# Reads for the range check, copies of the global keys, and the sums of second weights: three new places in the order of a sparse attention and FFN kernel

## The chip, the core and the metric

The kernel runs on one core of one Trainium2 chip. A core has TensorE (PE, with its weight loads PEld), VectorE (DVE), ScalarE (ACT), GpSimd (POOL) and SyncE (SP), which issues the DMAs here. The metric is the time of one execution on the device, in microseconds. Before the change it was 600.35 us, the median of three runs (599.40, 600.35 and 600.36). The execution that was profiled took 599.55 us.

## The reference, cut to what matters

```python
# attention: q, k, v of (4, 8, 768, 64); n_global = 8, n_local = 96
scores = np.matmul(q, k.transpose(0, 1, 3, 2)) / np.sqrt(D)
rel = pos[:, None] - pos[None, :]
is_global = pos[None, :] < n_global
is_local = (rel >= 0) & (rel < n_local)
dist = np.where(is_global & ~is_local, n_local, np.abs(rel))
scores = scores - slopes[:, None, None] * dist      # slope 2 ** -(h + 1)
a = softmax(np.where(is_global | is_local, scores, -1e9))
x = np.matmul(a, v)                                  # heads side by side: (4, 768, 512)
# feed-forward with a layer norm and a residual; w_ch1 is 512 x 2048, w_ch2 is 2048 x 512
xn = (x - mean(x)) / np.sqrt(var(x) + 1e-6) * g_ln
out = x + np.maximum(xn @ w_ch1, 0.0) @ w_ch2
```

The weights are float64 in HBM, all else is float32.

## The kernel before

**Tiles and chunks.** There are 24 tiles of 128 positions. Tiles 0 to 3 are the first tile of each batch element, tiles 4 to 8 are the other five of the first batch element in the list, and so on to tile 23. A tile's attention comes in groups of two heads, g = 0 to 3 (tiles 0 to 3 have two groups of four). Two tiles make a chunk of the feed-forward, c = 0 to 11. All float32 operands of the large products are split into a high and a low fp16 half, and a product is the sum of three fp16 products.

**The steps of a tile t, with the names that the tasks and the profile use.** S{t}_{g} on PE writes the scores (s <- kT,qT). R{t}_{g} on DVE adds the mask and takes the maxima (T <- s,mask, then nm). E on ACT takes the exponentials (mn, T). ph on ACT and pl on DVE or POOL make the two halves (pn), pt is a DMA transpose (pT <- pn), and P{t}_{g} on PE multiplies by the values (pv <- vn,pT). X divides (x <- pv,r), B squares the centred x on ACT (mean, xs), A and W on DVE and POOL make the root (rs), and C writes the centred and scaled x (xs <- x,mean,rs). xh on ACT and xl on DVE split it (xn), and xa is the DMA transpose to xT. The last 16 positions that every tile sees are the global ones: gk copies 16 columns of the first tile's keys into the block before the tile (kT <- kT on DVE), and gv does so for the values by DMA (vn <- vn).

**The steps of a chunk c.** F{c}_{f} on PE is the first product (f <- xT,w1h and w1l), G (chunks 0 to 2) and N (chunks 3 to 11) are the second. From chunk 3 on the second product is made of seven products of half size. For these, hr on ACT and hm on DVE mix the first product's results (R <- f, then R <- f,R three times), hh and hl make the halves (uh, ul), and sums of second weights are needed once: ya30, ya31, ya32 and so on add blocks of the weights (va <- va,w2l and the like) on DVE or POOL, yh and yl write the sum's halves (t <- va). There are four sets of these sums, the last digit of the key. D adds the results to x (x <- m,x), O stores them.

**The check of the weights.** After the work on tile 23 has begun, 64 reads V0 to V63 (again <- moe_w_ch, 256 KB each) bring the weights in once more, and J0 to J63 on DVE fold their exponents into one tile (seen). V{n} waits for tile 23's second scores and for a buffer; the three kinds of buffers are those of the loads (six), of the keys (three) and of the values (three). The verdict JJ follows J63, and one small product on PE (pf) takes it up near the end.

**What sets the order.** All tasks of the program are handed to a planner (`Plan`, lines 150 to 245). A task has a cost for each engine that may do it, the tasks it comes after, a rank, the buffers it takes and from which tasks they come back, and for a DMA its cost on the queue. The planner simulates the engines with these costs, and at every step takes the task that can begin first; among those that can begin within 0.05 us it takes the lowest rank. Where DVE, ACT or POOL may do a task, the one that would end it first by the planner's costs gets it. What comes out is one fixed order for each engine. On the chip every engine works through its own order, and waits at an instruction until its semaphores are reached. So one new constraint changes the choices behind it, the choice of engine too. SP waits in the same way: a read or a transpose that stands behind a waiting one is issued later. Each of SP's DMAs also waits for the landing of the eighth before it, whose semaphore it uses again.

All instructions are recorded through one helper, so every row of the profile has line L257; the names of the tiles tell them apart.

## Time and profile before

| | |
|---|---|
| median of the runs | 600.35 us |
| the profiled execution | 599.55 us, of which the span from the first to the last instruction is 597.8 us |
| TensorE | busy 586.9 us, 98% of the span, at a granted clock of 1.00 |
| VectorE | busy 494.0 us, 83% |
| ScalarE | busy 429.3 us, 72% |
| GpSimd | busy 154.0 us, 26% |
| DMA | mean 176 GB/s |

The profiled execution is 0.80 us below the median and 0.15 us above the fastest run. In a timeline row the first number is the start in us from the span's start, the second the duration, xN the instructions merged into the row, and in brackets stands how long the engine had been idle and what ended that. SPq is SP's queue: the duration of a row there is the issue of a DMA, not its transfer. The ends of matrix products are modelled, so a wait of PE of less than about 0.15 us does not show.

### The profile page before, as it was taken

The numbers are of one execution on the slowest core, as the hardware profiler recorded it, in microseconds if no ns is written. First come the engines' busy times: TensorE is split into PE (matmuls) and PEld (weight loads), VectorE is DVE, ScalarE is ACT, GpSimd is POOL, SyncE is SP. The second block draws the span as 40 slices with busy tenths as digits, with TensorE's granted clock in tenths as the row PEclk, the third lists the DMA queues.
The fourth block names the chain that finished last, engine by engine and source line by source line (L and its number), as shares of the span: only waits on it lengthen the run. The fifth ranks groups of instructions, "written<-read, shape, count | busy, mean of one in ns | idle before, by whom it ended". The sixth has DMA issues, their size and how long they took to land. (4 is left out here: it accounts for less than half of the span.)

```text
span 597.8 us, 15687 instructions
## 1 busy us (share of the span) xinstructions
PE 586.9 (98%) x5982; PEld 494.9 (83%) x5982; DVE 494.0 (83%) x1207; ACT 429.3 (72%) x1092; POOL 154.0 (26%) x133
## 2 busy tenths in 40 slices
PE   8999999999999999999999999999999999999996
PEld 5768895547956899999999999999999999888885
DVE  3899999989898987887887886877976876699994
ACT  5999697767666897797787698899686675623330
POOL 2322032135363253231330130231330420300100
PEclk9999999999999999999999999999999999999999
DMA  8995989999966848797776789759569646999931
GB/s 218 332 311 134 249 202 271 248 173 194 181 135 124 187 89 147 159 166 159 169 115 127 138 154 169 174 121 175 111 140 170 118 91 72 233 280 278 393 107 39
DMA packets 256754, 105.40 MB, mean 176 GB/s; under 512 B 238372, under 2 KB 238628, under 8 KB 256676
## 3 DMA queue, kind: packets, MB, share of 16 engines
q1 hardware_dynamic: 256672, 104.37, 78.1%
q8 instruction: 48, 0.79, 0.5%
q14 instruction: 30, 0.25, 0.1%
q10 hardware_dynamic: 4, 0.00, 0.0%
HBM read 54.53 MB, written 6.29 MB: 102 GB/s over the span
## 5 line engine op out<-in xcount | busy, mean ns | idle before, releaser
L257 PE MATMUL f<-xT,w1h 128*128 128x256 f16 x1536 | 256.3, 273 | 1.6 <-DMA xT<-xn 0.9
L257 PE MATMUL f<-xT,w1l 128*128 128x256 f16 x768 | 209.3, 273 | 0.0
L257 PEld LDWEIGHTS <-w1h 128*128 128x128 f16 x1536 | 147.3, 98 | 18.0 <-DMA xT<-xn 1.1
L257 ACT ACTIVATE uh<-R 128x896 f16<-128x896 f32 x72 | 67.9, 943 | 51.8 <-DVE R L257 50.3
L257 PEld LDWEIGHTS <-uh 128*128 128x128 f16 x1008 | 96.2, 98 | 10.5
L257 DVE SCALAR_TENSOR_TENSOR R<-f,R 128x128 f32<-128x128 f32 (+1 forms) x216 | 72.1, 334 | 20.6 <-ACT R L257 15.6
L257 PEld LDWEIGHTS <-w1l 128*128 128x128 f16 x768 | 75.1, 98 | 9.6 <-issue 0.7
L257 ACT ACTIVATE T<-T,mn 128x256 f32<-128x256 f32 x160 | 80.0, 500 | 4.3 <-ACT mn L257 0.4
L257 DVE TENSOR_TENSOR ul<-R,uh 128x896 f16<-128x896 f32 x60 | 68.1, 1136 | 17.0 <-ACT uh L257 15.9
L257 POOL TENSOR_TENSOR pn<-T,pn 128x512 f16<-128x512 f32 x37 | 49.9, 1349 | 120.2 <-ACT pn L257 82.4
L257 PE MATMUL m<-w2h,uh 128*128 128x256 f16 x288 | 78.5, 273 | 0.0
L257 PE MATMUL m<-w2l,uh 128*128 128x256 f16 x288 | 78.5, 273 | 0.0
L257 PE MATMUL m<-w2h,ul 128*128 128x256 f16 x288 | 78.5, 273 | 0.0
L257 PE MATMUL m<-t,uh 128*128 128x256 f16 x432 | 78.3, 273 | 0.0
L257 DVE CUSTOM_DVE_ANT_0 T<-s,mask 128x256 f32<-128x256 f32 (+1 forms) x192 | 68.1, 395 | 8.6 <-PE s L257 8.6
L257 PE MATMUL f<-w2h,h 128*128 128x512 f16 x192 | 60.1, 379 | 0.0
L257 PE MATMUL m<-t,ul 128*128 128x256 f16 x216 | 58.9, 273 | 0.0
L257 PE MATMUL s<-kT,qT 128*128 128x128 f16 (+1 forms) x704 | 56.9, 225 | 0.7 <-DVE kT L257 0.7
L257 PEld LDWEIGHTS <-ul 128*128 128x128 f16 x504 | 49.3, 98 | 5.7
L257 ACT ACTIVATE mn<-nm 128x2 f32<-128x2 f32 x80 | 15.8, 198 | 53.2 <-DVE nm L257 52.9
L257 POOL TENSOR_TENSOR rs<-rs,half 128x1 f32<-128x1 f32 x24 | 18.2, 760 | 138.1 <-DVE rs L257 138.0
L257 PEld LDWEIGHTS <-h 128*128 128x128 f16 x288 | 27.3, 98 | 29.7
(144 smaller groups left out, 994.6 us busy)
## 6 DMA issues: line engine op xcount, KB each, us to landing
again<-in_moe_w_ch_dram SPq DMA_DIRECT2D x64, 256.0 KB, 5.1
st<-in_moe_w_ch_dram SPq DMA_DIRECT2D x10, 1024.0 KB, 6.0
vf<-in_v_dram SPq DMA_DIRECT2D x28, 256.0 KB, 3.4
kf<-in_k_dram SPq DMA_DIRECT2D x28, 256.0 KB, 4.0
qf<-in_q_dram SPq DMA_DIRECT2D x24, 256.0 KB, 3.7
out_dram<-x SPq DMA_DIRECT2D x23, 256.0 KB, 3.6
qT<-qT SPq DMA_DIRECT2D x40, 128.0 KB, 3.5
w2h<-in_moe_w_ch_dram SPq DMA_DIRECT2D x3, 1024.0 KB, 6.6
```

Of the source, the lines that this page charges most:

```text
L257: ins = getattr(self.engine, name)(*args, **kw)
```

## The change

Three constraints of the planner are changed; no instruction is added or taken away by the diff itself.

```diff
@@ the planner's tables and Plan.task
+BEHIND = {"ya32_0": ["C5"], "yl3_0": ["C5"], "ya20_0": ["xl5"]}
...
-        self.tasks[key] = costs, fn, [a for a in after if a is not None], rank, take or {}, dma, slack, isinstance(engine, dict), port
+        self.tasks[key] = costs, fn, [a for a in [*after, *BEHIND.get(key, ())] if a is not None], rank, take or {}, dma, slack, isinstance(engine, dict), port
@@ the copy of the global keys
-                task(f"gk{b}_{i}", "DVE", 0.11, spread_k, [f"S{t - 1}_3"], rank=rank - 20, port=True)
+                task(f"gk{b}_{i}", "DVE", 0.11, spread_k, [f"S{t - 1}_3"], rank=rank - 200, port=True)
@@ the reads for the range check
-        task(f"V{n_}", "SP", 0.6, lambda n_=n_, tag=tag: read_again(n_, tag), [f"S{B * NT - 1}_1"], rank=1e4 + n_, take={tag: [f"J{n_}"]}, dma=0.8)
+        task(f"V{n_}", "SP", 0.6, lambda n_=n_, tag=tag: read_again(n_, tag), [f"S{B * NT - 1}_1"] + ([f"J{n_ - 12}"] if n_ >= 12 else []), rank=1e4 + n_, take={tag: [f"J{n_}"]}, dma=0.8, slack=2.5 * (n_ >= 12))
```

The sums ya32_0 and yl3_0 may no longer come ahead of tile 5's centred x, nor ya20_0 ahead of its low half. The copies gk get a lower rank, so they come first among what can begin. Reads from V12 on are planned 2.5 us after the J that frees their buffer.

VectorE's order from the low half of tile 6's last group on (pn6_3), before:

```order
L257 TENSOR_TENSOR pn6_3_1809<-T6_3_1749,pn6_3_1809 128x2x256
L257 TENSOR_TENSOR va0_1813<-va0_1813,w2l_86 128x512 x2
L257 TENSOR_TENSOR t3_1764<-va0_1813,t3_1764 128x2x256
L257 TENSOR_SCALAR xs5_1802<-x5_1795,mean_1803,rs_1811 128x512
L257 TENSOR_TENSOR va0_1813<-va0_1813,w2h_85 128x512
L257 TENSOR_TENSOR va0_1813<-va0_1813,w2l_86 128x512
L257 TENSOR_TENSOR xn5_1864<-xs5_1802,xn5_1864 128x512
L257 SCALAR_TENSOR_TENSOR x2_620<-f2_2_1374,x2_620 128x512
```

and now:

```order
L258 TENSOR_TENSOR pn6_3_1809<-T6_3_1750,pn6_3_1809 128x2x256
L258 TENSOR_TENSOR va0_1813<-va0_1813,w2l_86 128x512
L258 TENSOR_TENSOR va1_1845<-w2h_85 128x512
L258 TENSOR_SCALAR xs5_1802<-x5_1795,mean_1803,rs_1811 128x512
L258 TENSOR_TENSOR va0_1813<-va0_1813,w2l_86 128x512
L258 TENSOR_TENSOR xn5_1851<-xs5_1802,xn5_1851 128x512
L258 TENSOR_TENSOR t3_1762<-va0_1813,t3_1762 128x2x256
L258 TENSOR_TENSOR va0_1813<-va0_1813,w2h_85 128x512
```

The centred x of tile 5 (xs5) has moved ahead of the second addition to va0, and its low half (xn5) ahead of t3 and of two more additions. A first addition for the next set (va1), which was GpSimd's, now stands before xs5.

VectorE's order from the mixes of chunk 3's first product on (R from f1_3_0), where T9_3 is tile 9's last scores, before:

```order
L257 SCALAR_TENSOR_TENSOR R_1765<-f1_3_0_2766,R_1765 128x2x128
L257 SCALAR_TENSOR_TENSOR R_1765<-f1_3_0_2766,R_1765 128x128 x2
L257 TENSOR_TENSOR pn9_2_2833<-T9_2_2791,pn9_2_2833 128x2x256
L257 TENSOR_TENSOR w2l_86<-va2_2731,w2h_85 128x2x256
L257 TENSOR_TENSOR xn8_2804<-xs8_2715,xn8_2804 128x512
L257 ISA T9_3_2900,nm_2583<-s9_3_2863,mask1_88 128x256
L257 ISA nm_2583 128x1
L257 ISA T9_3_2900,nm_2583<-s9_3_2863,mask1_88 128x256
L257 ISA nm_2583 128x1
L257 SCALAR_TENSOR_TENSOR R_1765<-f1_3_2_2806,R_1765 128x2x128
L257 SCALAR_TENSOR_TENSOR R_1765<-f1_3_2_2806,R_1765 128x128 x2
L257 COPY kT9_1_2255<-kT09_0_2182 128x8x16
```

and now:

```order
L258 SCALAR_TENSOR_TENSOR R_1763<-f1_3_0_2749,R_1763 128x2x128
L258 SCALAR_TENSOR_TENSOR R_1763<-f1_3_0_2749,R_1763 128x128 x2
L258 TENSOR_SCALAR rs_2831<-mv_95 128x1
L258 SCALAR_TENSOR_TENSOR vn11_3_2829<-vf1_3_2774,vn11_3_2829 128x8x64
L258 COPY kT9_1_2407<-kT09_0_2171 128x8x16
L258 SCALAR_TENSOR_TENSOR R_1763<-f1_3_2_2793,R_1763 128x2x128
L258 SCALAR_TENSOR_TENSOR R_1763<-f1_3_2_2793,R_1763 128x128 x2
L258 ISA T9_3_2897,nm_2574<-s9_3_2851,mask1_88 128x256
L258 ISA nm_2574 128x1
L258 ISA T9_3_2897,nm_2574<-s9_3_2851,mask1_88 128x256
L258 ISA nm_2574 128x1
L258 TENSOR_SCALAR xs8_2819<-x8_2787,mean_2820,rs_2831 128x512
```

The mixes of the second product (R from f1_3_2) stood behind T9_3 and stand ahead of it now; halves and sums that stood between have gone elsewhere.

SP's order from the read V5 (again5) on, with tile 23's last two transposes (pT23_2 and pT23_3), before:

```order
L257 DMA again5_8465<-in_moe_w_ch1_dram 128x256
L257 DMA again12_8470<-in_moe_w_ch1_dram 128x256
L257 DMA again14_8473<-in_moe_w_ch1_dram 128x256
L257 DMA again7_8476<-in_moe_w_ch1_dram 128x256
L257 DMA_TRANSPOSE pT23_2_8489<-pn23_2_8467 128x8x128
L257 DMA again9_8521<-in_moe_w_ch1_dram 128x256
L257 DMA again13_8523<-in_moe_w_ch1_dram 128x256
L257 DMA again16_8556<-in_moe_w_ch1_dram 128x256
L257 DMA again17_8559<-in_moe_w_ch1_dram 128x256
L257 DMA again18_8569<-in_moe_w_ch1_dram 128x256
```

and now:

```order
L258 DMA again5_8465<-in_moe_w_ch1_dram 128x256
L258 DMA again7_8472<-in_moe_w_ch1_dram 128x256
L258 DMA_TRANSPOSE pT23_2_8475<-pn23_2_8467 128x8x128
L258 DMA again9_8511<-in_moe_w_ch1_dram 128x256
L258 DMA again12_8519<-in_moe_w_ch1_dram 128x256
L258 DMA again13_8521<-in_moe_w_ch1_dram 128x256
L258 DMA again14_8554<-in_moe_w_ch1_dram 128x256
L258 DMA again16_8559<-in_moe_w_ch1_dram 128x256
L258 DMA again17_8582<-in_moe_w_ch1_dram 128x256
L258 DMA out_0_dram<-x18_6721 128x512
L258 DMA again18_8613<-in_moe_w_ch1_dram 128x256
L258 DMA out_0_dram<-x19_7213 128x512
```

The transpose pT23_2 stood behind four reads and stands behind two. The reads V12 and V14 have moved behind it, and all that stood ahead of pT23_3 still does.

Of the tasks that the diff does not name, 30 change between DVE and POOL, all between the sums of the first set and tile 10. From tile 7's third scores to the mixes of chunk 3's first product DVE gains 15 tasks (ya41_0, yl4_0, ya31_2, ya32_2, yl3_2, kl10_2, pl8_1, ya30_3, ya41_2, ya10_0, ya10_2, yl3_3, ya12_2, yl1_2, ya21_3) and loses 10 (pl7_1, ql9, kl9_1, pl8_0, ya20_2, yl2_2, C7, A8, C8, kl11_3), some to POOL, some to an earlier or later place on DVE. POOL has three tensor operations fewer there. On PE the products P8 and P9 stand one place later among the larger ones, so P9_1 now follows the third product of chunk 3 (F3_4) instead of preceding it.

## Rows read from the trace of the kernel before

**Rows 1.** The page's head and its first part: busy us, share, instructions.

```profile
span 597.8 us, 15687 instructions
...
PE 586.9 (98%) x5982; PEld 494.9 (83%) x5982; DVE 494.0 (83%) x1207; ACT 429.3 (72%) x1092; POOL 154.0 (26%) x133
```

**Rows 2.** Waits of PE: us in total, times, longest us.

```profile
PE pv L257 <- DMA pT<-pn: 1.0, 2, 0.5
PE f L257 <- DMA xT<-xn: 0.9, 1, 0.9
PE s L257 <- DVE kT L257: 0.7, 1, 0.7
```

**Rows 3.** Timeline around the copy of the global keys for tile 6.

```profile
110.70 0.42 DVE L257 CUSTOM_DVE_ANT_0 T<-s,mask 128x256 f32<-128x256 f32 x1
...
111.39 0.19 DVE L257 COPY kT<-kT 128x128 f16<-128x128 f16 x1
...
111.64 0.22 PE L257 MATMUL s<-kT,qT 128*128 128x128 f16 x1 [0.70 <-DVE kT L257]
```

**Rows 4.** Timeline from tile 5's centred x to chunk 2's first product.

```profile
129.75 2.25 DVE L257 TENSOR_TENSOR va<-va,w2l 128x512 f32<-128x512 f32 x2
...
133.29 0.54 DVE L257 TENSOR_SCALAR xs<-x,mean,rs 128x512 f32<-128x512 f32 x1
...
133.87 0.63 ACT L257 ACTIVATE xn<-xs 128x512 f16<-128x512 f32 x1 [1.22 <-DVE xs L257]
...
135.08 0.68 DVE L257 TENSOR_TENSOR xn<-xs,xn 128x512 f16<-128x512 f32 x1
...
135.79 1.23 SPq L257 DMA_TRANSPOSE xT<-xn  x1
...
140.50 0.39 PE L257 MATMUL f<-xT,w1h 128*128 128x256 f16 x2 [0.93 <-DMA xT<-xn]
```

**Rows 5.** Windows: us, busy of PE, PEld, DVE, ACT, POOL, then clock, DMA.

```profile
144.10:195.20 51.10, 51.10 (x496) 37.35 (x495) 46.95 (x98) 36.37 (x103) 24.14 (x20) 1.00 0.82 158
```

**Rows 6.** Groups on DVE, 144.1 to 195.2: busy us, mean ns, idle before.

```profile
L257 DVE TENSOR_TENSOR va<-va,w2l 128x512 f32<-128x512 f32 x8 | 7.3, 913 | 0.1
L257 DVE TENSOR_TENSOR pn<-T,pn 128x512 f16<-128x512 f32 x7 | 7.1, 1019 | 1.3 <-ACT pn L257 1.2
```

**Rows 7.** Timeline of DVE, PE and ACT at chunk 3's first mixes.

```profile
195.19 1.07 DVE L257 SCALAR_TENSOR_TENSOR R<-f,R 128x256 f32<-128x256 f32 x3
...
198.67 1.07 DVE L257 SCALAR_TENSOR_TENSOR R<-f,R 128x256 f32<-128x256 f32 x3
...
197.85 0.58 ACT L257 ACTIVATE R<-f 128x512 f32<-128x512 f32 x1
...
196.32 0.39 PE L257 MATMUL f<-xT,w1h 128*128 128x256 f16 x2
...
198.95 0.38 PE L257 MATMUL f<-xT,w1h 128*128 128x256 f16 x2
```

**Rows 8.** Timeline of SP's queue and PE at tile 23's transposes.

```profile
518.76 2.75 SPq L257 DMA_DIRECT2D again<-in_moe_w_ch_dram  x4
521.61 1.30 SPq L257 DMA_TRANSPOSE pT<-pn  x1
...
528.45 1.28 SPq L257 DMA_TRANSPOSE pT<-pn  x1
...
525.85 0.52 PE L257 MATMUL pv<-vn,pT 128*128 128x64 f16 x12 [0.49 <-DMA pT<-pn]
...
533.58 0.52 PE L257 MATMUL pv<-vn,pT 128*128 128x64 f16 x12
```

**Rows 9.** Windows, columns as in rows 5: DMA share and GB/s come last.

```profile
526.00:529.00 3.00, 3.00 (x38) 2.72 (x36) 2.76 (x8) 0.00 (x0) 0.00 (x0) 1.00 1.01 307
```

**Rows 10.** Timeline of the verdict's last step on DVE and PE's product.

```profile
579.30 0.16 DVE L257 TENSOR_REDUCE mask<-ok 128x1 f32<-128x8 f32 x1
...
584.16 0.21 PE L257 MATMUL pf<-mask,ones 128*1 128x27 f32 x2
```

## The prediction

> **What bounds the kernel now.** I read the page's first part first: PE is busy in 98% of the span, 586.9 of 597.8 us [rows 1], so only what PE waits for can be won. The windows next: in the two stretches quoted here PE is busy from end to end, at a granted clock of 1.00, the 2.4 GHz level [rows 5, 9], and the windows over the rest of the span after the start read the same, so the clock has nothing to give back. Then the waits of PE. After the start-up the table holds four: 0.70 us once for DVE's copy of the global keys, 0.93 once for a transpose xT, and two of nearly 0.5 for transposes pT [rows 2]. They add up to 2.6 us, 0.4% of the time, and each of the three edits aims at one kind. The two pT waits belong to tile 23, one for its second group of two heads and one for its third [rows 8]. So the whole change has a ceiling of 2.6 us, and the question is what the moved instructions make late in exchange. The profiled run took 599.55 us, 1.75 more than its span and 0.80 less than the median of 600.35; I take gains from the profile and set them against the median.
>
> **Copies of the global keys.** Before tile 6's scores, DVE's order has two custom operations of tile 5's last range (T from s) and then the copy; the first begins at 110.70, the copy runs at 111.39 for 0.19, and PE goes on at 111.64 after 0.70 idle [rows 3]. With the copy first, it can begin at 110.70, so PE goes on at 110.95: 0.69 of the 0.70 is gained. The two custom operations end 0.19 later; behind them on DVE queue the next halves, and ACT's exponentials wait for them, but no wait of PE for pT shows there [rows 2]. Bounds: 0.5 (if the copy's input, not its place, held it by 0.2) to 0.70; taken 0.70. The copies of the other tiles have no wait in PE's table, so earlier or later they are worth 0 until one falls behind its scores.
>
> **The centred x of tile 5.** In the trace DVE runs the last two additions to va as one row of 2.25 us from 129.75, then a half (t), then xs at 133.29, 0.54 long; ACT makes the high half after 1.22 idle, DVE the low half at 135.08 for 0.68, SP issues the transpose at 135.79, and PE takes it up at 140.50 after 0.93 idle [rows 4]. Ahead of xs now goes one addition fewer (2.25 / 2 = 1.1), and t (1.1 between 132.0 and 133.29), and one first addition more (0.7 to 0.9 by [rows 6]): xs moves 1.3 to 1.5 earlier if its inputs are there. The low half then has one addition behind xs, not two, and waits for ACT's high half (0.63, [rows 4]), which begins with xs done. In all the issue comes 1.4 to 2.8 earlier. From the issue at 135.79 to PE's start passes 4.7 us; with the first edit's 0.70 PE wants the product at 140.50 - 0.93 - 0.70 = 138.9, and the transpose is there at 137.7 to 139.1. So the 0.93 goes, but for 0.2 at the worst end. Bounds 0.7 to 0.93, taken 0.93; the two edits give **1.63**, if nothing behind gives it back.
>
> **What the planner moves with it.** The thirty tasks that change between DVE and GpSimd are the dearest part. From 144.1 to 195.2 DVE is busy 46.95 of 51.10 us [rows 5], 4.15 idle. It gains 15 tasks there, mostly halves and additions, and loses 10. Such tasks last 0.68 alone (the low half in [rows 4]) and 0.91 to 1.02 on the mean in this stretch [rows 6], where GpSimd runs 20 operations beside them. Five more at 0.66 to 0.84 are 3.3 to 4.2 us. Against that GpSimd does three tensor operations fewer; if what the means lie above 0.68 comes from running beside it, each of its operations costs DVE 0.25 to 0.5, so 0.7 to 1.5 come back. Net +1.8 to +3.5 us of work, 2.6 between them. All of it must be done before the first mixes of chunk 3 (R from f, 1.07 at 195.19), whose bank PE wants at 196.32 [rows 7]. In the new order PE is 1.63 ahead, and the product P9_1 (twelve products, about 0.4 of PE's time by [rows 8]) has gone behind; so the bank is wanted at 196.32 - 1.63 - 0.4 = 194.3, and DVE must begin by 193.2. The stretch also begins earlier, at 144.1 - 1.3 = 142.8, since its first operation follows scores of PE (two tasks, 0.3 us by their overlap, now stand ahead of it). So 46.95 + 2.6 = 49.55 us of work stand in 50.4 us, and 0.85 of the 4.15 us of idle time may stay; 1.65 with the small end, nothing with the large one. The moved additions and halves of weights wait for nothing on PE, and some of the idle time is a wait for ACT (1.3 in front of the seven low halves, [rows 6]) in which they fit. Bounds: a loss of 0 (the idle time fills) to 4.2 (all stays, with the large end). Taken **0**, also because up to 0.7 lost here would be lost right behind it anyway:
>
> There the order of VectorE has tile 9's last range (T9_3) behind the second mixes instead of ahead of them, and the range frees the bank for the product that PE begins at 198.95, now wanted at 197.3 [rows 7]. The mixes wait for ACT's part (R from f at 197.85, 0.58 long [rows 7]), which ended at 198.43. By its order ACT loses two halves and a mask's copy ahead of that part and gains a square: about one half less, 0.63 [rows 4]. So the part ends at 196.2 if it also follows PE's 1.63, and at 197.8 if ACT stays where it was. Behind it come the mixes, 1.07, and the range, two custom operations of 0.42 less an overlap of some 0.05: the bank is free at 198.0 to 199.6, and PE is held for 0.7 to 2.3; 0 if the halves on ACT turn out 0.7 earlier still, as they do when VectorE's previous range comes early. Taken **-0.7**, the case in which ACT follows PE, because its input is PE's; 0.1 more for the third product's bank.
>
> **Reads for the range check.** SP's queue issues four reads in 2.75 us from 518.76, 0.69 each, before the third transpose at 521.61 [rows 8]. Two of them now stand behind it, so it goes out 1.38 us earlier and lands that much earlier: its wait of 0.49 [rows 8] is gone. The second transpose's 0.46 stays, since ahead of it nothing changes. But the two reads have only moved behind the third transpose and still stand ahead of the fourth, which goes out at 528.45 [rows 8]; around it the DMA engines are at a share of 1.01, 307 GB/s [rows 9]. So the same bytes land before it, at the same time. PE took its fourth group at 533.58 with no wait that shows [rows 8]; arriving there 0.49 earlier, it waits 0.49. Net 0 (0 to 0.5), taken **0**. The trace says transfers come one after another there; that is what the 0 hangs on. The Trainium skill ("DMA: Bandwidth & Descriptors", section "Queues, rings and completion order") says that a later transfer may end before an earlier one, since completion isn't first in, first out per queue. By that rule the fourth transpose needn't wait for the moved reads' bytes, and the 0.49 would be kept; no row here shows one overtaking. At the end, the verdict's step on DVE is done at 579.46 and PE's product on it begins at 584.16 [rows 10]: 4.7 us cover what later reads delay there, so that costs 0, and would cost what exceeds 4.7.
>
> **Sum.** 0.70 + 0.93 - 0.70 - 0.10 + 0 = 0.83 us: 598.7 for a run like the profiled one, **599.5** against the median. With its bounds (gain 0.3 to 1.4) 599.0 to 600.1.
>
> **Rivals.** *The gains are kept.* ACT's part follows PE, the range of tile 9 costs nothing, perhaps the fourth transpose comes early too. For it speaks that the whole middle of the kernel moves with PE; against it that the range now ends behind the mixes, where it began before them [rows 7]. Gain 1.6 to 2.1, so 598.7 to 598.2, taken 598.6.
>
> *VectorE is overloaded, and it is slower.* In 144 to 195 DVE keeps the idle time it has, because it sits in waits for ACT and PE at the points where the order now has nothing else ready. Then the mixes begin 4.15 - 0.85 = 3.3 later than wanted, and PE's third product of chunk 3 with them, which takes the 1.63 and 1.7 more; the range then costs nothing of its own: 602.0, and 602.9 with the large end. In general PE loses what stays of the 4.15 beyond 0.85; the case is slower than before once more than 2.5 stays, slower by over 1.2 us from 3.7 on (2.9 with the large end). For it speaks the 92% that DVE is busy; against it that additions and halves of the weights wait for nothing on PE. The Trainium skill ("GPSIMD Engine Reference", section "8. Key points") says that GpSimd shares its ports to the memory with VectorE and that instructions of VectorE with two inputs there contend with it. By it three fewer operations on GpSimd would speed DVE up; the rows agree as far as means of 913 and 1019 ns beside 680 go, and this rival would need the opposite.
>
> *The change does not reach its wait, or all is eaten.* The transpose xT stays late, as its 4.7 us from issue to use are mostly queue and not issue, or the range at 198.95 takes 1.6: gain 0 to 0.3, 600.2.
>
> **How the numbers follow.** Forecast 0.44 (599.5); gains kept 0.32 (598.6); overloaded 0.15 (602.0; under 601 where less than 3.2 of the idle time stays, for which I take a third); not reached 0.09 (600.2). About 0.2%, 1.2 us, is what a measurement of this kernel can tell from no change. Faster by over 1.2 us: the gains kept (0.32) and 0.03 from the forecast's upper end: 0.35. Slower by over 1.2: 0.09 of the overloaded rival and 0.06 for a loss of 2.3 or more at the range: 0.15. Within: 0.50. The range runs from 598.2 (all kept, the fourth transpose too) to 601.0 (the loss of 2.3 at the range, or the small overload), and leaves out about 0.1 above and less below.
>
> **What would show it.** In the profile after: PE's waits without the 0.7 for kT and the 0.9 for xT (if not, steps one and two are wrong); the transpose of tile 5's x issued at 133 to 134.5; DVE busy for 49 to 50.5 us from 142.8 to 193.5; a new wait of PE for DVE near 197 of about 0.7 (larger than 1.5 and with DVE behind at the first mixes: the overload; none: the gains kept); the two pT waits at the second and fourth group of tile 23, not the second and third; no wait at pf. A loss elsewhere in the middle, or an xT of a later chunk that comes late, would make the prediction wrong.

## The result, and the profile after

The changed kernel is slower: 604.68 us, the median of six runs (601.71 to 607.01), against 600.36 for the kernel before in runs beside it (599.40 to 601.93). The ratio is 1.0073, with an interval of 1.0049 to 1.0097. The forecast of 599.5 was wrong, and the time lies above its range; what happened is in its outline the rival that VectorE is overloaded, priced at 602.0. The profiled execution of the changed kernel is the fastest of the six, 601.71 us with a span of 599.9, so the traces show 2.16 us of the difference between two executions, and the medians 4.3.

The page's head and first part, as in [rows 1]: VectorE has gained 2.1 us of busy time and GpSimd lost 5.3 over the whole span.

```profile
span 599.9 us, 15691 instructions
...
PE 586.0 (98%) x5982; PEld 494.4 (82%) x5982; DVE 496.1 (83%) x1211; ACT 429.2 (72%) x1092; POOL 148.7 (25%) x129
```

The waits of PE, as in [rows 2] (us in total, times, longest; what belongs to the start-up is left out):

```profile
PE pv L258 <- DVE mv L258: 1.5, 1, 1.5
PE pv L258 <- DMA pT<-pn: 1.3, 2, 0.8
PE f L258 <- ACT R L258: 0.9, 1, 0.9
PE s L258 <- DVE kT L258: 0.8, 1, 0.8
...
PE f L258 <- DVE rs L258: 0.5, 1, 0.5
...
```

Of the four waits of before, the one for tile 5's xT is gone. The one for kT is still there. Of the pT row, 0.46 belongs to tile 23 as before and 0.82 to tile 15, at 350. New are one of 1.5 for tile 8's division (mv), one of 0.5 that the view puts down to rs, and one of 0.9 for ACT's R. All three lie between 193 and 205.

**The copy of the global keys.** Tile 6's copy now stands ahead of the custom operations, as the diff says, and yet PE waits as long as in [rows 3]:

```profile
111.06 0.18 DVE L258 COPY kT<-kT 128x128 f16<-128x128 f16 x1
111.16 0.41 DVE L258 CUSTOM_DVE_ANT_0 T<-s,mask 128x256 f32<-128x256 f32 x1
...
111.30 0.48 PE L258 MATMUL s<-kT,qT 128*128 128x128 f16 x5 [0.77 <-DVE kT L258]
```

The copy begins at 111.06, not at 110.70. This execution was 0.54 us ahead of the one of before when the start-up ended (PE's first product of chunk 0 begins at 43.41, there at 43.95). Counted from there, VectorE is about 1 us later than in the kernel before all the way from 86 to 112, and the delay begins in one place, tile 5's copy, which the same edit moved forward as well. Timeline of the changed kernel there, GpSimd first, then VectorE:

```profile
84.81 2.07 POOL L258 TENSOR_TENSOR kn<-kf,kn 128x512 f16<-128x512 f32 x1 [6.53 <-ACT kn L258]
...
85.78 1.16 DVE L258 COPY kT<-kT 128x128 f16<-128x128 f16 x1
```

In the kernel before, tile 5's copy came when GpSimd had finished (88.81, its operation having ended at 87.49):

```profile
88.81 0.18 DVE L257 COPY kT<-kT 128x128 f16<-128x128 f16 x1
```

The same 16 columns per head took 0.18 there and 1.16 here, and the copy ends when GpSimd's operation does (86.94 and 86.88).

**The centred x of tile 5.** VectorE's timeline, to be read against [rows 4]:

```profile
131.29 0.54 DVE L258 TENSOR_SCALAR xs<-x,mean,rs 128x512 f32<-128x512 f32 x1
131.75 1.64 DVE L258 TENSOR_TENSOR va<-va,w2l 128x512 f32<-128x512 f32 x1
133.32 1.64 DVE L258 TENSOR_TENSOR xn<-xs,xn 128x512 f16<-128x512 f32 x1
134.88 1.64 DVE L258 TENSOR_TENSOR t<-va,t 128x512 f16<-128x512 f32 x1
```

The centred x comes 2.0 earlier, but three operations behind it take 1.64 each instead of 0.68, so the transpose is issued at 134.98, only 0.81 earlier. GpSimd runs three additions beside them, from 131.52 to 135.97. PE takes the product up at 139.08 without a wait, 1.42 earlier than before; 0.54 of each of these times is the shorter start-up.

**From 144 to 205.** The window that answers to [rows 5], from the same operation to the first mixes of chunk 3, in the same columns:

```profile
144.14:195.56 51.42, 49.89 (x484) 36.05 (x482) 48.05 (x104) 36.13 (x102) 20.85 (x17) 1.00 0.85 157
```

VectorE has 1.1 us more work in six more operations; 3.4 us of idle time are left. The window begins where it began before (144.10), although PE is 1.42 ahead, and ends 0.36 later. Before, VectorE stood idle there until PE's scores came:

```profile
DVE T L257 <- PE s L257: 0.9, 1, 0.9
```

Now it has no such wait: the scores wait for VectorE, which the three long operations have made late. VectorE's own waits in this window say where it idles:

```profile
DVE pn L258 <- ACT pn L258: 1.3, 2, 1.1
DVE w2l L258 <- ACT w2h L258: 0.8, 1, 0.8
DVE R L258 <- ACT R L258: 0.5, 1, 0.5
DVE rs L258 <- ACT xs L258: 0.4, 1, 0.4
```

All are waits for ACT, 3.0 together, and all but the R's 0.5 come before 179.1; from there to the mixes VectorE runs almost without a gap. VectorE, ACT and PE near its end, to be read against [rows 7]:

```profile
192.26 0.41 DVE L258 CUSTOM_DVE_ANT_0 T<-s,mask 128x256 f32<-128x256 f32 x1
...
194.37 0.69 DVE L258 CUSTOM_DVE_ANT_1 x<-pv,r 128x512 f32<-128x512 f32 x1
194.98 0.08 DVE L258 DVE_READ_ACCUMULATOR2_ANT mv<- 128x1 f32 x1
195.56 1.08 DVE L258 SCALAR_TENSOR_TENSOR R<-f,R 128x256 f32<-128x256 f32 x3 [0.49 <-ACT R L258]
...
193.05 0.20 ACT L258 ACTIVATE mn<-nm 128x2 f32<-128x2 f32 x1 [3.62 <-DVE nm L258]
...
195.21 0.51 PE L258 MATMUL pv<-vn,pT 128*128 128x64 f16 x12 [1.53 <-DVE mv L258]
...
196.69 0.39 PE L258 MATMUL f<-xT,w1h 128*128 128x256 f16 x2 [0.52 <-DVE rs L258]
...
204.20 0.39 PE L258 MATMUL f<-xT,w1h 128*128 128x256 f16 x2 [0.95 <-ACT R L258]
```

Tile 9's third range (T9_2), whose scores were ready at 188.4, is reached by VectorE at 192.26; ACT sits idle for 3.62 until its maxima are there (2.25 before). Tile 8's division (x <- pv,r), which ran at 187.37 before, ahead of that range, runs at 194.37 behind it (its last row is the read of an accumulator, mv). It empties the bank that PE's next product of values (pv) needs: 1.53. The first mixes then wait for ACT's part of the same bank, and PE's third product for the mixes: 0.52. A last wait of 0.95 comes two products later, at the fifth. Its bank is the third product's, which VectorE's mixes at 203.08, 1.06 long, empty; the view names ACT's R, which ended within 0.05 us of them. Ahead of these mixes stand T9_3, tile 8's centred x and a low half (ul), the last two 1.18 and 2.05 long beside GpSimd. The wait forecast for the fourth product (0.7, for T9_3 behind the second mixes) did not come.

**Tile 23's transposes**, against [rows 8], SP's queue and PE:

```profile
521.24 1.00 SPq L258 DMA_DIRECT2D again<-in_moe_w_ch_dram  x2
522.35 1.88 SPq L258 DMA_TRANSPOSE pT<-pn  x1
...
524.70 0.52 PE L258 MATMUL pv<-vn,pT 128*128 128x64 f16 x12 [0.46 <-DMA pT<-pn]
...
527.68 0.51 PE L258 MATMUL pv<-vn,pT 128*128 128x64 f16 x12
```

The second group waits 0.46 as before, the third no more, and the fourth not by anything that shows (0.02).

**The account.** Of PE's waits, 0.93 (xT), 0.49 (third transpose) and 0.10 at 510 went; 1.53, 0.52 and 0.95 came, and 0.95 in two transposes of tile 15 (343 to 350), 0.23 for an xT at 548, 0.07 at kT and 0.09 at a wait near 91. That is +2.8. The start-up was 0.54 us shorter, which leaves 2.2; the span grew by 2.1, and PE's last product comes 2.3 later. The start-up is not the change's doing: up to tile 5's copy at 85.8 every engine of both kernels has the same instructions in the same order. The granted clock is 1.00 in both profiles until PE's work is done.

### The profile page after: what moved, and what is told of

Its sections match the earlier page's. It is cut to its first block, busy times and chain, and to the rows that moved or that the text cites. A ratio compares the mean times of both kernels' runs of the same rounds, so it can differ in the third digit from the quotient of the medians.

```text
span 599.9 us, 15691 instructions
## 1 busy us (share of the span) xinstructions
PE 586.0 (98%) x5982; PEld 494.4 (82%) x5982; DVE 496.1 (83%) x1211; ACT 429.2 (72%) x1092; POOL 148.7 (25%) x129
## 4 chain that ended last, share of the span: by engine, by line
PE 50%; DVE 21%; ACT 9%; issue 6%; DMA 4%; POOL 1%; SPq 0%; DVEq 0%; ACTq 0%; POOLq 0%
PE f L258 23%; PE m L258 21%; PE s L258 3%; DVE st L258 3%; PE pv L258 3%; DVE T L258 2%; ACT T L258 2%; DVE w2l L258 2%; DVE x L258 2%; DMA again<-in_moe_w_ch_dram 2%; DVE h L258 2%; DVE va L258 2%; DVE R L258 1%; ACT uh L258 1%; DVE pn L258 1%
## 5 line engine op out<-in xcount | busy, mean ns | idle before, releaser
L258 ACT ACTIVATE R<-f 128x512 f32<-128x512 f32 x72 | 41.9, 582 | 14.4 <-PE f L258 14.2
```

The costliest lines, as they stand in the source:

```text
L258: ins = getattr(self.engine, name)(*args, **kw)
```

## The experiments

Two questions are put. Why is it slower: too much work on VectorE before chunk 3's mixes (the load), or the new order of single tasks (the division, T9_3, the fourth product), or the reads? And why did the copy gain nothing? The rivals to the load are the order, the reads, and a lowered clock of PE behind the new waits. In most kernels the planner's order is kept and named entries are moved within it; in these lists gk0_2 and gk0_3 are the copies for tiles 5 and 6, S, R, E, X, W, C, xh, xl, ya, yl, h, pt and so on the steps named above, and "behind" or "ahead" says on which side of the last name the first is put. Engines stay as they were. In what follows, "waits" are PE's, in us, and ratios are against the kernel before on the same chip.

### The change without its parts

`again` is the changed kernel once more, `no_reads` the change without its third edit:

```diff
-    ... [f"S{B * NT - 1}_1"] + ([f"J{n_ - 12}"] if n_ >= 12 else []), ..., slack=2.5 * (n_ >= 12))
+    ... [f"S{B * NT - 1}_1"], ...)
```

> The changed kernel once more, with no edit, for a second profile. Theory A (the planner's new order overloads VectorE between 144 and 195 us, so tile 8's division comes behind tile 9's third range and PE waits for it): the waits of PE for VectorE of 1.5, 0.5 and ACT/VectorE of 0.9 between 193 and 204 us come back, 2.5 to 3.5 us together, and the time is 602 to 605. Theory B (the loss sits in DMA: the later reads and late transposes): the waits for pT and xT are larger than in the first profile (1.5 together), and those for VectorE are not always there.

> The changed kernel without the edit of the range-check reads; the copies and the sums stay, and the order up to 510 us with them. Theory A: as slow as the changed kernel, plus 0 to 0.5 us (604.5 to 605.2 beside a before of 600.4). Theory B: the loss goes with the reads, 599 to 600.5.

`again` ran in 603.31, ratio 1.0066 [1.0041, 1.0091], with waits of 1.15, 0.52 and 0.95 at 194, 196 and 203 and 0.78 at kT; `no_reads` in 604.21, 1.0062 [1.0039, 1.0085], with 1.42, 0.53 and 0.96. The loss repeats, and the reads have no part in it that shows.

`only_reads` is the kernel before with the third edit alone.

> The kernel before with the edit of the range-check reads alone; the other engines keep their order up to 543 us. By the prediction the third transpose of tile 23 comes earlier and the fourth takes over its wait: 0 to 0.5 us faster, with waits of PE for pT near 521 and 533. Theory B: slower by 2 us or more.

It ran in 600.00, 1.0009 [0.9993, 1.0024]. The third transpose of tile 23 is not waited for any more, the fourth for 0.15; the second's wait had gone too in this execution, and other transposes were late (0.49 at 343, 0.95 at 350, 0.40 at 276). The reads edit moves the time by nothing that can be measured, as forecast, though not by the path forecast: of the 0.49 that was to come back at the fourth transpose, 0.15 came here, and 0.02, 0.23, 1.08 and 0.09 in the four profiles of the changed kernel (the first, `again`, `again_2`, `again_3`).

`only_sums` is the kernel before with the second edit alone (BEHIND), so the planner moves sums between engines but copies and reads stay.

> The kernel before with the edit of the sums alone, with the order that follows from it (54 tasks on another engine, in part up to tile 18). Theory (the new distribution between VectorE and GpSimd overloads VectorE before 195 us): waits of PE for VectorE between 165 and 205 us of 1.5 us or more together, and no faster than before (600.4 to 604). If the overload needs the edit of the copies too: no such waits over 0.5 together, and 0.5 to 1 us faster than before.

It ran in 604.87, 1.0072 [1.0049, 1.0096]: this edit alone loses as much as the whole change, though by another order. Its waits are not the same ones:

```profile
171.30 0.51 PE L258 MATMUL pv<-vn,pT 128*128 128x64 f16 x12 [1.77 <-issue]
...
184.27 0.52 PE L258 MATMUL pv<-vn,pT 128*128 128x64 f16 x12 [0.95 <-DMA pT<-pn]
...
191.22 0.52 PE L258 MATMUL pv<-vn,pT 128*128 128x64 f16 x12 [0.35 <-DMA pT<-pn]
...
201.66 0.39 PE L258 MATMUL f<-xT,w1h 128*128 128x256 f16 x2 [1.23 <-DVE R L258]
```

The view names no releaser for the 1.77, but VectorE shows it: tile 7's division ends with its read of the accumulator, 0.08 long from 171.12, and PE goes on at 171.30; at tile 8 in the changed kernel the pair was 194.98 and 195.21. So another plan of the same sums has the same kind of loss at another tile's division, and at chunk 3's mixes. It has more that the changed kernel lacks: 1.58 at 415.8 for a division's r and 0.81 at 530.9 for a transpose. So its loss and that of the change are alike in kind, and their equal size is partly chance.

### The two waits without the planner's moves

`two_places` moves in the kernel before only what the first two edits are for; `two_places_root` moves the root W5 as well. In `two_places` tile 5's centred x is scaled with the root of an earlier tile, since W5 stays behind it.

```diff
+AHEAD = [('gk0_3', 'R5_3'), ('C5', 'ya32_0'), ('xh5', 'ya32_0'), ('xl5', 'yl3_0')]
```

```diff
+MOVED = [("gk0_3", "ahead", "R5_3"), ("W5", "ahead", "ya31_0"), ("C5", "ahead", "ya32_0"), ("xh5", "ahead", "ya32_0"), ("xl5", "ahead", "yl3_0")]
```

> The kernel before, its order for every engine taken over as it stands, and two places in it moved by hand: tile 6's copy of the global keys ahead of tile 5's last range, and tile 5's centred x with its two halves ahead of the second addition to va and of the sum's half. No task changes its engine. Theory A: the two waits of PE (0.70 and 0.93) go and nothing else comes: 1.4 to 1.7 us faster, 598.7 to 599.0. Rival: the gain is given back within 10 us of each place whatever the engine of the sums, 600 to 600.4.

> Like two_places, but tile 5's centred x waits for its own root (in two_places it took the root that stood there from an earlier tile, so VectorE didn't wait there). The two places alone, no task on another engine. Theory A2 (the gain of 1.63 us carries PE ahead of VectorE, which has no idle time left before 195 us): the waits of 0.70 and 0.93 are gone, and waits of PE for tile 7's and tile 8's division, the transpose of tile 9's second scores or the mixes take 1 to 1.6 of it back by 197 us; time 599.0 to 599.9 beside a before of 600.0. Theory A1 (only the moved tasks cost, VectorE itself has room): the gain stays, 598.3 to 598.7.

`two_places` ran in 599.31, 0.9987 [0.9974, 1.0001]; `two_places_root` in 599.92, 0.9992 [0.9972, 1.0013]. In the latter the wait for kT is down to 0.07 and that for xT is gone, so the 0.70 and the 0.93 were rightly priced. But PE gives most of it back within 60 us. Its timeline from 188:

```profile
188.99 0.51 PE L265 MATMUL pv<-vn,pT 128*128 128x64 f16 x12 [0.38 <-DVE mv L265]
...
196.17 0.52 PE L265 MATMUL pv<-vn,pT 128*128 128x64 f16 x12 [0.99 <-DMA pT<-pn]
```

These 1.37 are waits for tile 8's division and for a transpose. VectorE makes the low half for that transpose at 190.84, 0.76 later than before (190.08), and the start-up of this execution was 0.73 longer (chunk 0's first product at 44.68): counted from there, VectorE keeps its old times. With no engine changed and no task added, a PE that is 1.6 earlier runs into VectorE's schedule. The changed kernel's repeats say the same: in `again` and `again_2` PE waits 0.27 and 0.54 right behind kT for a transpose of queries (qT), and its wait for the division is 1.15 and 0.97, not 1.53 or 1.56. What PE loses earlier, it does not wait for there. The ceiling of 2.6 us from PE's waits was therefore not a gain to be had from these places.

### Is it the load or the order?

`after_lighter` is the changed kernel without five of the additions to the sums, five times 0.68 us of VectorE's work at least; the sums lack those terms. `after_division` moves tile 8's division back ahead of tile 9's third range.

```diff
+LEFT_OUT = ("ya31_2", "ya32_2", "ya41_2", "ya11_2", "ya12_2")
...
-        return [fn for _, _, fn in order]
+        return [fn for key, _, fn in order if key not in LEFT_OUT]
```

```diff
+MOVED = [("X8", "ahead", "R9_2")]
```

> The changed kernel without five additions of the sums of second weights on VectorE between 147 and 190 us (ya31_2, ya32_2, ya41_2, ya11_2, ya12_2; the sums are incomplete, all else is computed as before): 3.4 to 4 us less work for VectorE there, no order changed. If VectorE's load is the cause: the waits of PE for the division and the mixes between 193 and 204 us (3.0 us) go but for at most 0.5, and it is 2.5 to 3 us faster than the changed kernel (601 to 602). If the order is the cause whatever the load: 2 us or more of the waits stay.

> The changed kernel with one task moved by hand: tile 8's division (x from pv), which frees the bank of the products P9_0, stands ahead of tile 9's third range instead of three tasks behind it. If the place of the division is the cause of the largest wait: the 1.2 to 1.5 us of PE for it go, the two waits of 0.5 and 0.95 behind it stay, 1.0 to 1.5 us faster than the changed kernel (602 to 603). If VectorE's backlog is the cause: the wait only moves to the next product that needs VectorE, and the sum of the waits between 190 and 205 us stays within 0.5 us of 3.0.

`after_lighter` ran in 600.32, 1.000 [0.9979, 1.0020]. The wait for the division is gone and that for the third product is 0.15:

```profile
196.36 0.39 PE L259 MATMUL f<-xT,w1h 128*128 128x256 f16 x2 [0.15 <-DVE rs L259]
...
203.87 0.39 PE L259 MATMUL f<-xT,w1h 128*128 128x256 f16 x2 [0.95 <-ACT R L259]
```

Of 3.0 us in three waits, 1.1 remain. Some 0.4 of what went is not the load: this execution has a wait of 0.38 for qT behind kT. And 3.4 us are three times what the change added to VectorE in the window. So the first two waits hang on how much work VectorE has ahead of them. The 0.95 at the fifth product does not: 3.4 us less work leave it as it was. For it the order is left, T9_3, the centred x and the low half ahead of the mixes, but no run moves these back.

`after_division` ran in 605.79, 1.0076 [1.0046, 1.0107], no better. Its waits of PE:

```profile
PE f L266 <- DVE rs L266: 2.8, 1, 2.8
```

The division's wait was only moved. Tile 9's third range, put behind the division, starts at 194.00; ACT's exponentials follow at 194.81, its part of the first mixes at 196.70 (194.95 before), and the third product pays 2.82 in place of 1.53 and 0.52. Both tasks are late, and neither order of the two helps: that is a lack of VectorE's time. The windows of this kernel from 195 on show something more (the clock is the column of 0.84):

```profile
195.00:200.00 5.00, 2.18 (x23) 1.55 (x19) 2.83 (x8) 4.90 (x14) 2.05 (x3) 0.84 0.65 171
200.00:205.00 5.00, 5.00 (x48) 4.13 (x47) 4.84 (x10) 4.68 (x15) 3.88 (x3) 0.82 0.67 105
```

After a wait of 2.82 PE was granted its 1.2 GHz level, not that of 2.4, in a part of each of these windows, 1.7 us of work by these two rows (5 x 0.16 + 5 x 0.18).

### Does the clock explain the longer executions?

In some executions the changed kernel takes 605 to 607, so two more profiles of it were taken, since a fall like the last would cost about what is missing.

> The changed kernel without an edit, one more profile, for the granted clock. Where PE has waited for about 2 us between 193 and 197 us, theory C (the waits lower the clock) expects a granted clock under 1.00 in the slices behind 195 us in the executions over 604 us, and 1.00 all along in those near 602. If the longer executions have a clock of 1.00 behind 195 us, their time comes from elsewhere (the start-up or transposes).

> As again_2, once more: over 604 us with a granted clock under 1.00 behind 195 us, or near 602 us with 1.00.

They took 604.25 and 601.77, with waits of 0.97, 0.52, 0.94 and 1.56, 0.53, 0.95 at 194 to 206, and a granted clock of 1.00 there in both. The clock is not what makes `again_2` longer. Its waits show what does: the start-up was 1.6 us longer (chunk 0's first product at 45.04, not 43.41), and transfers came later (qf below, one vn with 0.5 and one pT with 1.1).

```profile
PE s L258 <- DVE kT L258: 1.1, 1, 1.1
...
PE tq L258 <- DMA qf<-in_q_dram: 0.7, 1, 0.7
```

Over all executions the answer is another one, for the record has the mean granted clock of each. In three profiles the clock fell while PE had work (`no_reads`, `after_division`, `first_copy_back`): their means are 0.996 and 0.997, those of all other profiles 0.998 or more (a fall after PE's last work is in each mean). Of the 20 executions of the changed kernel and of `no_reads`, 10 have 0.997 or less, and their median is 605.3; the other 10 have 603.1. Of the 99 executions of the kernel before that ran beside the experiments, 11 have 0.997 or less, with 602.1 against 600.1 for the rest. So without a fall of the clock the change costs about 2.9 us, which is near the 2.8 of its waits, and the falls in half of its executions can make up the rest of the 4.3. Where the clock fell in executions without a profile is not known, and that the new waits caused it is not shown. In `no_reads` it fell in the start-up, behind waits of PE of 1.09 and 1.96 (PE's busy time, clock, DMA share, GB/s):

```profile
30.00:35.00 5.00, 3.83 (x19) 0.73 1.03 418
```

### Why the copy gained nothing

`first_copy` moves in the kernel before tile 5's copy alone to where the change has it; `first_copy_back` is the changed kernel with that one copy back in its old place.

```diff
+MOVED = [("gk0_2", "ahead", "R4_3")]
```

```diff
+MOVED = [("gk0_2", "behind", "wl9")]
```

> The kernel before with one move: tile 5's copy of the global keys ahead of tile 4's last range, where the changed kernel has it. If a copy beside GpSimd's long operation waits for it (theory): the copy lasts 1.1 to 1.2 us instead of 0.18, VectorE is 0.9 to 1.0 later up to tile 6's copy, PE's wait for that copy (0.70) becomes 1.5 to 1.7, and the time is 0.5 to 1.0 us longer. If VectorE's delay comes from elsewhere (loads that land late): the copy lasts 0.18, the wait stays 0.70 and the time is the same.

> The changed kernel with tile 5's copy of the global keys back where it was before the change (behind a weight half), all else as changed. Theory: the copy lasts 0.18, PE's wait of 0.8 at tile 6's copy goes to 0 to 0.2, the waits between 193 and 204 us stay at 2.4 to 3.2 since VectorE and PE both come earlier: 0.3 to 0.9 us faster than the changed kernel (603.0 to 604.2). If the lateness of VectorE there has another cause: the wait stays at 0.7 to 0.8.

`first_copy` ran in 601.90, 1.0024 [1.0004, 1.0043]. VectorE and PE in its timeline (GpSimd has the same operation on kn at 85.76, 2.07 long):

```profile
86.73 1.15 DVE L265 COPY kT<-kT 128x128 f16<-128x128 f16 x1
...
112.94 0.65 PE L265 MATMUL s<-kT,qT 128*128 128x128 f16 x8 [1.46 <-DVE kT L265]
```

The copy is stretched to 1.15 again, and tile 6's scores, 26 us later, are waited for 1.46 instead of 0.70: moving a 0.18 us copy of another tile costs 0.76. `first_copy_back` ran in 601.55, 1.0016 [1.0001, 1.0032]. Its copy takes 0.18, and PE begins tile 6's scores without a wait:

```profile
88.03 0.18 DVE L266 COPY kT<-kT 128x128 f16<-128x128 f16 x1
...
110.16 0.54 PE L266 MATMUL s<-kT,qT 128*128 128x128 f16 x6
```

The two kernels show both directions. The waits for the division and the third product stay (1.57 and 0.52), as the load has them. The window behind them again has a lowered clock, 0.66, which is 1.7 us of work (5 x 0.34):

```profile
195.00:200.00 5.00, 4.48 (x30) 3.33 (x29) 4.05 (x13) 4.68 (x13) 3.85 (x5) 0.66 0.80 142
```

The wait of 0.95 at the fifth product is missing in this profile and in that of `after_division`; in both PE comes to it later by about what the clock took, which may be all there is to it. The kernel gained more against the change (0.57% by the two ratios, 3.4 us) than the wait for kT of 0.8 explains; in the profiled executions the difference is 0.8 (600.92 and 601.71). The clock goes some way: 1 of its 12 executions has 0.997 or less (2 of 12 in `after_lighter`), against 10 of 20. Why it falls less often here is open.

### Can the gains be kept?

Three kernels take the two places with the root and the reads edit, and then move what was late next. In `five_places`:

```diff
+MOVED = [..., ("X7", "ahead", "vl9_1"), ("ql11", "behind", "X8"), ("pt15_2", "ahead", "qt17"), ("pt15_3", "behind", "pl15_3")]
```

`load_later` puts work that is not urgent behind the mixes of chunk 3, and `load_later_2` puts two of these tasks later still, and an addition (ya20_3) too:

```diff
+MOVED = [..., ("ya12_1", "behind", "X8"), ("yh1_1", "behind", "ph9_1"), ("ql11", "behind", "pl9_1"), ("yl1_1", "behind", "hm3_2"), ("vl10_2", "behind", "hm3_2"), ("pt15_2", "ahead", "qt17"), ("pt15_3", "behind", "pl15_3")]
```

```diff
-("yl1_1", "behind", "hm3_2"), ("vl10_2", "behind", "hm3_2")
+("yl1_1", "behind", "hl3_6"), ("vl10_2", "behind", "hm3_6"), ("ya20_3", "behind", "hm3_4")
```

> The kernel before with the edit of the reads and these moves by hand, no task on another engine: the two of two_places_root; tile 7's division ahead of a value half; the query half of tile 11 behind tile 8's division; on SP's queue tile 15's third transpose one place and its fourth two places earlier. Each move aims at a wait of PE of 0.2 to 0.6 us that appeared in two_places or in the runs of this study. If VectorE's backlog can be turned by order alone: 1.5 to 2.5 us faster than before, 597.5 to 598.5. If not: 599 to 600.

> The kernel before with the edit of the reads, the two places of two_places_root, the two earlier transposes of tile 15, and work of VectorE that nobody needs soon moved to later places by hand, no task on another engine: a sum (ya12_1) with its halves behind tile 8's division, tile 11's query half behind tile 9's second half, and a sum's half and a value half (2 x 0.7 us) from before tile 9's third range to behind chunk 3's second mixes. If VectorE's backlog before 195 us is what takes the gain back: no wait of PE over 0.3 between 180 and 205 us, 598.0 to 599.0 beside a before of 600.2. If the backlog only moves behind 195: 599.5 to 601 with new waits between 197 and 215 us.

> Like load_later, but what stood ahead of chunk 3's third mixes there (a sum's half, a value half, an addition) goes behind later mixes, where PE's products had 1.2 to 2.5 us of room in two_places_root. If VectorE's load in the right place keeps the gain: the wait of 2.0 at 201 us goes, no wait of PE over 0.4 between 180 and 230 us, 598.0 to 599.2 beside a before of 600.2. If not: new waits of more than 1 us together between 195 and 230 us.

They ran in 600.56, 0.9996 [0.9975, 1.0017]; 600.73, 1.0006 [0.9982, 1.0030]; and 601.30, 1.0010 [0.9994, 1.0027]. None beats the kernel before. In each, one row shows where the gain went:

```profile
182.93 0.52 PE L265 MATMUL pv<-vn,pT 128*128 128x64 f16 x12 [1.15 <-DMA pT<-pn]
```

```profile
203.12 0.39 PE L265 MATMUL f<-xT,w1h 128*128 128x256 f16 x2 [1.98 <-DVE R L265]
```

```profile
201.94 0.39 PE L265 MATMUL f<-xT,w1h 128*128 128x256 f16 x2 [0.62 <-DVE R L265]
...
225.29 0.52 PE L265 MATMUL pv<-vn,pT 128*128 128x64 f16 x12 [1.01 <-DMA pT<-pn]
```

In `five_places` it is a transpose at 182, and one more of 1.05 at 196; in `load_later` the moved work stands ahead of the third mixes, 1.98; in `load_later_2` 0.62 are left of that and two transposes at 225 and 231 take 1.01 and 0.63. Each time the gain is given back to another engine or a transpose before 240 us. In `load_later` the clock has a part too: 6 of its 12 executions have a mean of 0.997 or less, with a median of 602.9; the other six have 599.1, against 600.7 for the like executions of the kernel before on that chip. So few executions are a hint of a gain, not more.

## Why the prediction was wrong, step by step

- **What bounds the kernel: right, but read too far.** PE's four waits were the whole of its loss, and two of them were removable: `two_places_root` removed them. The step "so the whole change has a ceiling of 2.6 us" held; that the gains stay "if nothing behind gives it back" is where the size was lost. Even without the planner's moves 1.37 of 1.63 was lost again by 197.
- **Copies: the price was right, its side condition failed.** 0.70 is what the place was worth (`first_copy_back`: no wait). The step that failed is "the copies of the other tiles have no wait in PE's table, so earlier or later they are worth 0 until one falls behind its scores". Tile 5's copy cost 1.0 of VectorE's time not by being late but by meeting GpSimd, and the delay came out at tile 6.
- **Centred x: right in result.** The 0.93 went. The issue came 0.81 earlier, not 1.4 to 2.8, since three operations were stretched to 1.64 beside GpSimd; it sufficed because the wait for kT had stayed and PE came later. The row of 2.25 for two additions was halved to 1.1 each, but the trace has 0.69 for one and 1.53 for the other, which began beside a GpSimd operation; and t took 0.69 behind 0.69 of waiting for ACT, not 1.1. The stretching was in the row before the change, hidden by the mean.
- **What the planner moves: the failing step of the sum.** It was taken at 0 with bounds up to 4.2, and PE waited 2.05 for it (1.53 and 0.52). The work grew by 1.1, less than the 1.8 to 3.5 reckoned (47.85 us in 142.8 to 193.5, forecast 49 to 50.5), and the idle time shrank from 4.15 to 3.4. But the stretch did not begin 1.3 earlier: it began at 144.14, since VectorE was late from 131 to 136 and no longer waited there for PE; so VectorE had no more room than before while PE came earlier. The sum's range, a gain of 0.3 to 1.4, did not carry the bounds of this term or the 2.3 of the next. "0.85 of the idle time may stay" was right as a rule, and 3.4 stayed; the idle time did not fill, since it lies in waits for ACT, early in the stretch, that the moved additions did not fill. The reason given for 0, that additions wait for nothing on PE, is true and does not matter, because they stand ahead of tasks that PE waits for.
- **Tile 8's division: not seen.** Its move behind tile 9's third range stands in the order and was not priced; it is the largest single wait, 1.53. `after_division` shows that its place alone is not to blame.
- **T9_3 behind the second mixes: wrong place.** Forecast 0.7, measured 0. The fourth product begins at 199.67, before the range has ended (200.09), so in the new order it doesn't take the range's bank; the second mixes, which end at 199.41, are what had just come free. The third product's 0.1 was 0.52, and the fifth product's 0.95 was not forecast; `after_lighter` leaves it as it was, so it is not the load before 195.
- **Reads: right, at 0.** `only_reads` is within what can be measured. The way there is uncertain: by the prediction the fourth transpose would wait 0.49, and it waited 0.02, 0.09, 0.15, 0.23 and 1.08 in five profiles. The rule of the Trainium skill that the prediction weighed ("DMA: Bandwidth & Descriptors", section "Queues, rings and completion order") allows the small values, but no row shows one transfer passing another, and the 1.08 speaks against keeping the gain.
- **The rivals.** "VectorE is overloaded" named the place, the first mixes of chunk 3. Its 602.0 lies near the 601.71 of the profiled execution by luck: it was reckoned from the median, +1.65, against +2.16 between the profiles and +4.3 between the medians. Its point, more than 2.5 of idle time left, was passed (3.4). Two things in it were not as written: it reckoned the whole loss there, and it took the 1.63 as gained first; in the trace 0.93 was gained, 2.05 lost to the load and 0.95 at the fifth product. It was given 0.15. What should have raised that is in [rows 5] and [rows 6]: 92% busy and VectorE's idle time in waits for ACT. The argument against it, that sums wait for nothing, spoke of the wrong tasks.
- **What stays open.** The medians differ by 4.3, the profiles by 2.16. The waits at 193 to 206 are in every profile of the change; the rest varies between executions. Those of the changed kernel spread over 601.7 to 607.0 in the first comparison. `again_2`, 604.25, is late at the start-up and in transfers, and half of the executions have a lowered clock, against one in nine of the kernel before. The prediction had the clock at 1.00 throughout and no term for it. Why it is lowered more often there is open.

## What to carry to other kernels

Before pricing a wait of the bounding engine as a gain, look at how much room the engines that feed it have over the next tens of microseconds: with VectorE 92% busy, a TensorE that came 1.6 us earlier only waited elsewhere. Where a scheduler shifts tasks from GpSimd to VectorE, follow the tasks whose end releases a PSUM bank or starts ScalarE, the divisions and ranges, not the tasks that were shifted. And a short copy moved forward can cost more than it saves when it lands beside a GpSimd operation: look at what GpSimd is doing at the new time, for all the instances that the edit moves, not just the one with the wait.

## What the runs showed of the hardware

- **VectorE beside GpSimd.** A copy of fp16 that takes 0.18 us alone took 1.16 and 1.15 beside a GpSimd operation with two inputs, and ended with it; two-input operations on VectorE of 0.68 took 1.64. The custom operation T <- s,mask, which reads scores from PSUM, took its usual 0.41 in the kernel before at 86.39, in the middle of GpSimd's operation there (85.41 to 87.49). The Trainium skill ("GPSIMD Engine Reference", section "8. Key points") says that GpSimd shares its SBUF interfaces with VectorE, and contends with VectorE's instructions that have two SBUF inputs or run in a 2-port perf mode. The trace agrees for the two-input operations, and shows the copy, which has one input, end only with GpSimd's operation, twice; which mode the copy ran in no row shows.
- **The clock after a wait.** The granted clock was 0.84 and 0.82 in the two windows of 5 us around and after a wait of 2.82, 0.66 in the window after waits of 1.57 and 0.52 in another kernel, and 0.73 in the start-up of `no_reads` around a wait of 1.96; in the profiles of the changed kernel, with waits of 0.97 to 1.56 and then 0.52, it stayed at 1.00. What decides between them was not tested.
